# Normalized cross-covariance attention and a multiplicative FFN: the first batch's loads in another order, the last outputs in two PSUM tiles

## The chip, the cores and the metric

The kernel runs on one core of a Trainium2 chip. The metric is the device time of one execution in microseconds (us). Seven executions of the kernel before the change took 575.99 to 577.0 us, median 576.5. All times in the text are in us unless they are marked ns.

The engines are named as in the profile: PE multiplies matrices (PEld is its loading of weights), DVE and ACT do elementwise work, POOL issues the loads that convert float32 to bfloat16, and SP issues the stores and the transposing transfers. A suffix q (SPq, ACTq) marks an engine's queue of transfers.

## The reference

Four batches (B = 4) of q, k and v, each 5824 x 256 in float32. In outline:

```python
qn = q / (norm(q, axis=1) + 1e-6)          # norm of each of the 256 columns, over 5824 rows
kn = k / (norm(k, axis=1) + 1e-6)
s = kn.transpose(0, 2, 1) @ qn / tau       # 256 x 256 per batch, tau = 1
a = softmax(s, -1)
x = (v @ a).reshape(4 * 5824, 256)
h = (x @ w1) * (x @ w2) @ w3               # w1, w2: 256 x 1024; w3: 1024 x 1024
out = h @ w_out                            # w_out: 1024 x 256
```

So the 256 x 256 matrix a of a batch needs every row of its q and k, and only then can the rows of v be worked on.

## The kernel before

**Algebra and tiles.** The rows of a batch lie on 128 partitions, 45 slots to a partition (5760 rows), and 64 rows are left over. A slot is a 128 x 256 tile. Eight slots make a piece: pieces 0 to 4 are full, piece 5 has 5 slots and, for q and k, the 64 left rows in a sixth slot (LAST = 5), padded with zeros. The kernel folds a into the weights: Wf = a @ [w1, w2] per batch, and W_sb = w3 @ w_out once. For each chunk of 512 rows (c = 0 to 10) and each 128 of the 1024 hidden columns (j = 0 to 7), `emit_ab` makes two matmul groups a and b out of the transposed v and Wf (L424), ACT copies a out of PSUM (L430), DVE multiplies it with b (L439). `emit_out` multiplies the product by W_sb[j] and sums over j in PSUM (L463); at j = 7 ACT and DVE copy the sums out (L483, L484) and SP stores them (L485). Chunk 11 of each batch is small: the 45th slot (128 rows) and the 64 left rows. The left rows of two batches are put together as one 128-row tile, so batches 1 and 3 have two output tiles of 128 x 256 in chunk 11, and batches 0 and 2 have one. In the kernel before both lie in one PSUM tile (L459); ACT copies the first half (L473), DVE the second (L476), and the left rows are stored by two transfers of 64 rows each (L479).

**PSUM.** Tag "ab" has four buffers, tag "out" three, "G" one. A chunk takes two "out" tiles in turn, so a chunk's second tile takes the buffer of the first tile of the chunk before.

**The first batch.** Nothing can run beside it, so its order is written out by hand (L496 to L565). POOL loads the pieces of q and k in the order of `load_piece` calls; each transfer also waits until the one eight places ahead of it has landed. PE makes, per slot, the squares of k (`squares`, L221; the diagonal of k^T k gives k's norms), those of q, and the products G = q^T k (`products`, L233). `busy` issues matmuls on a tile of zeros that nothing reads (L209). The softmax is in units, `soft0`:

- `k_first` (L244): DVE takes the diagonal of k's squares into dk.
- `k_row` (L272 to L277): PE spreads the k norms to a row; ACT makes kr, the inverse norm, in four operations.
- `q_first` (L251): DVE takes the q sums into ss.
- `scaled_first`: DVE scales half of G by kr (L302), ACT and DVE make r from ss (L291 to L294), DVE scales the other half, ACT makes e = exp(r * s) in two operations (L307).
- `first_folds`: PE sums e (L323), DVE makes the inverse rs (L329, L330), and PE makes folds 0 to 5 (L344), 128 x 512 each; ACT evicts the even ones (L351) and DVE the odd ones (L353), scaled by rs, into Wf. Folds 0 to 3 are needed by j = 0 to 3, folds 4 to 7 by j = 4 to 7. Folds 6 and 7 come between the first matmuls of the main loop.

The first half of v's piece 0 is transposed by PE (L132), copied out by DVE (L136), and stands ahead of `first_folds`. After the q and k pieces POOL loads the halves of w1 and w2 (L539, L540) between the halves of v_0, then v_1, v_2, w_out (L546) and w3 (L547).

**Later batches.** Loads, squares, products and softmax of batch n + 1 are spread over batch n by an agenda of due times (`make_agenda`); `gate` and `hold` keep POOL from issuing loads too early.

The functions that the change touches, and what calls them:

Of the kernel before, what the change touches and what calls it, by code (L numbers as in the profile page):

```python
# [12 lines left out]
F32 = DT.float32  # L13
BF16 = DT.bfloat16

P = 128
# [8 lines left out]
def kernel(  # L25
# [12 lines left out]
    nc = tc.nc  # L38

    B, N, C = q.shape  # L40
    T, D = out.shape
# [8 lines left out]
    FT = F // P  # L50
    NT = N // P
    LEFT = N - NT * P
    assert LEFT == 64 and NT % 4 == 1
    NP_ = (NT + PIECE - 1) // PIECE
    LAST = NT - (NP_ - 1) * PIECE
# [11 lines left out]
    work = ctx.enter_context(tc.tile_pool(name="work", bufs=2))  # L67
    psum = ctx.enter_context(tc.tile_pool(name="psum", bufs=1, space=bass.MemoryType.PSUM))
# [16 lines left out]
    W_sb = consts.tile([P, FT, D], BF16)  # L85
# [14 lines left out]
    def new_piece(nm, n, pi):  # L100
        t = in_pool.tile([P, PIECE, C], BF16, tag=nm, name=f"{nm}_{n}_{pi}", bufs=IN_BUFS[nm])
        pieces[nm, n, pi] = t
        if pi == NP_ - 1:
            if nm != "v":
                nc.vector.memset(t[LEFT:, LAST, :], 0.0)
            nc.gpsimd.dma_start(out=t[:LEFT, LAST, :], in_=qk_main[nm, n][1])

    def load_part(nm, n, pi, lo, hi):
        nc.gpsimd.dma_start(  # L109
            out=pieces[nm, n, pi][:, lo:hi, :], in_=qk_main[nm, n][0][:, pi * PIECE + lo : pi * PIECE + hi, :]  # L110
        )

    def load_piece(nm, n, pi, cuts=()):

        new_piece(nm, n, pi)
        ends = [0, *cuts, LAST if pi == NP_ - 1 else PIECE]
        for lo, hi in zip(ends, ends[1:]):
            load_part(nm, n, pi, lo, hi)
# [3 lines left out]
    def new_vT(n):  # L122
        vTs[n] = (
            vT_pool.tile([P, NT - 1, CT, P], BF16, tag="vT", name=f"vT_{n}"),
            vT_pool.tile([P, CT, P + LEFT], BF16, tag="vTt", name=f"vTt_{n}"),
        )
# [11 lines left out]
    def transpose_half_on_pe(n, pi, h, on_act):  # L138
        if pi == 0 and h == 0:
            new_vT(n)  # L140
        t = pieces["v", n, pi]
        i0 = 4 * h
        pe_transpose(
            vTs[n][0][:, pi * PIECE + i0 : pi * PIECE + i0 + 4, :, :].rearrange("p i c t -> p (i c) t"),
            [t[:, i0 + i, ct * P : (ct + 1) * P] for i in range(4) for ct in range(CT)],
            "out", on_act,
        )
# [57 lines left out]
    def busy(k):  # L205

        m = psum.tile([P, 512], F32, tag="ab", name=f"warm_{nc.get_next_instruction_name()}", bufs=4)
        for _ in range(k):
            nc.tensor.matmul(m, lhsT=warm[:, :P], rhs=warm, start=True, stop=True, skip_group_check=True)  # L209
# [3 lines left out]
    def squares(nm, pi, slots, end=False):  # L213

        if nm not in S:
            S[nm] = psum.tile([P, CT, P], F32, tag="out", name=f"sq{nm}_0", bufs=3)
        t = pieces[nm, 0, pi]
        for i in slots:
            for ct in range(CT):
                cs = slice(ct * P, (ct + 1) * P)  # L220
                nc.tensor.matmul(  # L221
                    S[nm][:, ct, :], lhsT=t[:, i, cs], rhs=t[:, i, cs],
                    start=(pi == 0 and i == 0 and ct == 0),
                    stop=(end and i == slots[-1] and ct == CT - 1), skip_group_check=True,
                )

    def products(pi, slots, end=False):
        if 0 not in G_tiles:
            G_tiles[0] = psum.tile([P, CT, C], F32, tag="G", name="G_0", bufs=1)
        qt, kt = pieces["q", 0, pi], pieces["k", 0, pi]  # L230
        for i in slots:
            for ct in range(CT):
                nc.tensor.matmul(  # L233
                    G_tiles[0][:, ct, :], lhsT=qt[:, i, ct * P : (ct + 1) * P], rhs=kt[:, i, :],
                    start=(pi == 0 and i == 0 and ct == 0),
                    stop=(end and i == slots[-1] and ct == CT - 1), skip_group_check=True,
                )

    def soft_units(n):
# [94 lines left out]
            sum_mm(0)  # L334
            sum_mm(1)

        def fold_mm(i, c2, tag="ab"):
            h, rest = divmod(i, 4)
            w, c1 = divmod(rest, 2)
            if c2 == 0:  # L340
                st["fold", i] = psum.tile(
                    [P, 512], F32, tag=tag, name=f"fold_{n}_{i}", bufs={"ab": 4, "out": 3}[tag]
                )
            nc.tensor.matmul(  # L344
                st["fold", i], lhsT=st["e"][:, c2, c1 * P : (c1 + 1) * P], rhs=w12[:, c2, w, h * 512 : (h + 1) * 512],
                start=(c2 == 0), stop=(c2 == CT - 1),
            )
            if c2 == CT - 1:
                dst = Wf[n][:, c1, w, h * 512 : (h + 1) * 512]
                if i % 2 == 0:  # L350
                    nc.scalar.activation(out=dst, in_=st["fold", i], func=AF.Copy, scale=st["rs"][:, c1 : c1 + 1])  # L351
                else:
                    nc.vector.tensor_scalar_mul(dst, st["fold", i], st["rs"][:, c1 : c1 + 1])  # L353

        def fold(i, tag="ab"):
            fold_mm(i, 0, tag)
            fold_mm(i, 1, tag)

        def first_folds():
            sum_mm(0)  # L360
            fold_mm(0, 0)
            fold_mm(1, 0)
            sum_mm(1)
            fold_mm(0, 1)
            fold_mm(1, 1)
            fold(2)
            fold(3)
            fold(4, "out")
            fold(5, "out")

        if n == 0:
# [77 lines left out]
    def emit_out(b, c, j, ab):  # L449
        small = c == NCH - 1  # L450
        if small:
            lhs = [ab[:, :P]]
            if b % 2 == 1:
                lhs.append(lefts[b // 2][:, j, :, :].rearrange("p b t -> p (b t)"))
        else:
            lhs = [ab[:, i * P : (i + 1) * P] for i in range(4)]
        if j == 0:
            out_tiles[b, c] = [
                psum.tile([P, 2, D], F32, tag="out", name=f"o_{b}_{c}_{h}", bufs=3) for h in range((len(lhs) + 1) // 2)  # L459
            ]  # L460
        tl = out_tiles[b, c]
        for s, lhsT in enumerate(lhs):
            nc.tensor.matmul(  # L463
                tl[s // 2][:, s % 2, :], lhsT=lhsT, rhs=W_sb[:, j, :],
                start=(j == 0 and s % 2 == 0), stop=(j == FT - 1 and (s % 2 == 1 or s == len(lhs) - 1)),
                skip_group_check=True,
            )
        clock[0] += len(lhs) * (D * MM_COL + MM_FIX)
        if j == FT - 1:
            o = work.tile([P, 4, D], F32, tag="o_sb", name=f"osb_{b}_{c}", bufs=3)  # L470
            rows = out[b * N : b * N + NT * P, :].rearrange("(p i) c -> p i c", i=NT)
            if small:
                nc.scalar.copy(o[:, 0, :], tl[0][:, 0, :])  # L473
                (nc.scalar if b == B - 1 else nc.sync).dma_start(out=rows[:, NT - 1, :], in_=o[:, 0, :])
                if b % 2 == 1:
                    nc.vector.tensor_copy(o[:, 1, :], tl[0][:, 1, :])  # L476
                    for k in range(2):
                        m = b - 1 + k
                        nc.sync.dma_start(  # L479
                            out=out[m * N + NT * P : (m + 1) * N, :], in_=o[k * LEFT : (k + 1) * LEFT, 1, :]  # L480
                        )
            else:
                nc.scalar.copy(o[:, 0:2, :], tl[0])  # L483
                nc.vector.tensor_copy(o[:, 2:4, :], tl[1])  # L484
                nc.sync.dma_start(out=rows[:, 4 * c : 4 * c + 4, :], in_=o)  # L485
            del out_tiles[b, c]
# [8 lines left out]
    half = PIECE // 2  # L495
# [20 lines left out]
    for pi in range(1, 4):  # L516
        load_piece("k", 0, pi)
        load_piece("q", 0, pi)
    load_piece("k", 0, 4)
    load_piece("k", 0, 5)  # L520
    soft0 = soft_units(0)
    whole = range(PIECE)
# [6 lines left out]
        products(0, sl)  # L529
    for pi in range(1, 4):  # L530
        squares("k", pi, whole)
        busy(2)
        squares("q", pi, whole)
        products(pi, whole)
    load_piece("q", 0, 4, (half,))
    load_piece("q", 0, 5, (2, 4))
    for h in range(2):
        hs = slice(h * F // 2, (h + 1) * F // 2)
        nc.gpsimd.dma_start(out=w12[:, :, 0, hs], in_=w1r[:, :, hs])  # L539
# [6 lines left out]
    nc.gpsimd.dma_start(out=wout_sb, in_=moe_w_out.rearrange("(lh ll) c -> ll lh c", ll=P))  # L546
    nc.gpsimd.dma_start(out=w3_bf, in_=w3r)  # L547
    squares("k", 4, whole)
    squares("k", 5, range(LAST + 1), end=True)
    soft0[0]()  # L550
    busy(2)
    soft0[1]()
    for sl in (lo, hi):
        squares("q", 4, sl)
        products(4, sl)
    parts = [[LAST, 0, 1], [2, 3], [4]]
    for sl in parts:
        squares("q", 5, sl, end=sl is parts[-1])
        if sl is parts[-1]:
            soft0[2]()  # L560
        products(5, sl, end=sl is parts[-1])
    soft0[3]()
    busy(4)
    transpose_half_on_pe(0, 0, 0, False)
    soft0[4]()  # L565
    w_ready = [False]

# [114 lines left out]
```

## Time and profile before

| | us |
|---|---|
| median of seven executions | 576.5 |
| the profiled execution, whole time | 577.43 |
| its span, first to last recorded instruction | 575.7 |
| PE busy | 562.2 (98%) |
| DVE, ACT, POOL busy | 374.5, 338.2, 65.1 |
| first matmul of the main loop (L424) | near 40.5 |
| last output matmul ends | 571.16 |
| last store issued | near 572.6 |

How to read the lines: a row in order of time gives start, duration, engine, line of the kernel, operation, output <- input with shapes, the number of instructions merged (x12), and in brackets how long the engine sat idle just before and what ended that. In a list of waits a row gives who waited for whom, the sum in us, how often, and the longest. A row of the chain of waits gives start, duration and the group that set the time. In the DMA view a queue's row gives packets, MB, and the time of its packets as a share of 16 engines over the window; an issue's row gives KB each and the us from issue to landing.

### The profile page before, as it was taken

To read this page: it belongs to the slowest core of one execution; us is meant where nothing else is said; L and a number is where in the kernel's file an instruction comes from. 1 tells how busy PE (TensorE), PEld (TensorE's weight loads), DVE (VectorE), ACT (ScalarE), POOL (GpSimd) and SP (SyncE) were. 2 spreads that over 40 slices of the span, in tenths; PEclk is the share of its full clock that TensorE was granted. 3 is DMA by queue.
4 is the path that set the end of the run, shared out by engine and by line. 5 is a ranking of instruction groups with operands and counts; after the bars stand their busy time and mean duration, and the time that the engine had idled before them with its cause. 6 is when DMAs were issued, how large, how long until landed. Compare 5 with 4: busy or idle time off the path is not lost.

```text
span 575.7 us, 10111 instructions
## 1 busy us (share of the span) xinstructions
PE 562.2 (98%) x3762; PEld 357.3 (62%) x3770; DVE 374.5 (65%) x597; ACT 338.2 (59%) x624; POOL 65.1 (11%) x147
## 2 busy tenths in 40 slices
PE   8799999999999999999999999999999999999996
PEld 4665576776666566666666666666665656566665
DVE  0047744787967567887776567778876656565564
ACT  0046534777766477776765567767765554454453
POOL 5240020202100111011000112001100000000000
PEclk9999999999999999999999999999999999999999
DMA  8999969969571999564642799654563335311011
GB/s 164 211 208 199 185 112 217 186 159 223 129 176 47 139 176 210 113 145 93 144 110 77 149 215 178 147 111 88 147 138 81 84 79 145 84 41 71 38 74 55
DMA packets 74416, 76.93 MB, mean 134 GB/s; under 512 B 54144, under 2 KB 58112, under 8 KB 74368
## 3 DMA queue, kind: packets, MB, share of 16 engines
q0 software_dynamic: 15360, 39.46, 39.9%
q1 hardware_dynamic: 58864, 36.71, 22.6%
q8 instruction: 29, 0.48, 0.4%
q14 instruction: 19, 0.16, 0.1%
q10 hardware_dynamic: 144, 0.13, 0.1%
HBM read 78.91 MB, written 23.86 MB: 179 GB/s over the span
## 4 chain that ended last, share of the span: by engine, by line
PE 88%; DMA 7%; ACT 1%; issue 1%; DVE 1%; POOL 1%; ACTq 0%; POOLq 0%
PE a L424 27%; PE o L463 26%; PE b L424 26%; PE G L188 5%; DMA q<-in_q_dram 4%; DMA k<-in_k_dram 2%; PE fold L344 2%; PE w L571 1%; DMA v<-in_v_dram 1%; ACT as L430 1%; POOL k L109 0%; DVE abs L439 0%; DVE osb L484 0%; PE row L272 0%; POOL q L109 0%
## 5 line engine op out<-in xcount | busy, mean ns | idle before, releaser
L439 DVE TENSOR_TENSOR abs<-as,b 128x512 bf16<-128x512 bf16 x336 | 229.6, 685 | 141.7 <-ACT as L430 130.5
L430 ACT CAST as<-a 128x512 bf16<-128x512 f32 (+1 forms) x384 | 215.4, 562 | 178.1 <-PE a L424 87.7
L424 PEld LDWEIGHTS <-Wf 128*128 128x128 bf16 x1536 | 149.1, 98 | 102.2 <-issue 2.3
L463 PE MATMUL o<-W_sb,abs 128*128 128x256 bf16 x1376 | 209.6, 273 | 0.5 <-ACT osb L483 0.4
L424 PE MATMUL a<-vT,Wf 128*128 128x512 bf16 x704 | 209.3, 379 | 0.4
L424 PE MATMUL b<-vT,Wf 128*128 128x512 bf16 x704 | 209.4, 379 | 0.0
L463 PEld LDWEIGHTS <-abs 128*128 128x128 bf16 x1376 | 134.5, 98 | 82.0 <-issue 0.6
L197 DVE TENSOR_TENSOR acc<-acc,sq 128x1024 f32<-128x1024 f32 x66 | 80.4, 1219 | 0.8 <-ACT sq L185 0.8
L188 PE MATMUL G<-k,q 128*128 128x256 bf16 x276 | 49.6, 273 | 1.1 <-DMA k<-in_k_dram 1.1
L412 POOL COPY gate_t<-abs 1x1 bf16<-1x1 bf16 x39 | 9.7, 248 | 300.7 <-DVE abs L439 292.1
L185 ACT ACTIVATE sq<-q 128x512 f32<-128x512 bf16 x66 | 41.8, 633 | 0.0
L185 ACT ACTIVATE sq<-k 128x512 f32<-128x512 bf16 x66 | 41.6, 630 | 0.0
L484 DVE COPY osb<-o 128x512 f32<-128x512 f32 x44 | 30.1, 684 | 0.0
L188 PEld LDWEIGHTS <-q 128*128 128x128 bf16 x276 | 27.0, 98 | 4.5 <-issue 1.4
L483 ACT COPY osb<-o 128x512 f32<-128x512 f32 x44 | 25.7, 585 | 4.6 <-PE o L463 2.6
L274 ACT ACTIVATE kr<-row 128x256 f32<-128x256 f32 x4 | 1.5, 384 | 31.0 <-PE row L272 31.0
L109 POOL DMA_DIRECT2D q<-in_q_dram x28 | 15.0, 538 | 14.0 <-DMA k<-in_k_dram 5.2
L344 PE MATMUL fold<-w,e 128*128 128x512 bf16 x61 | 16.3, 378 | 0.1
L351 ACT ACTIVATE Wf<-fold,rs 128x512 bf16<-128x512 f32 x16 | 10.9, 687 | 7.2 <-PE fold L344 4.3
L109 POOL DMA_DIRECT2D k<-in_k_dram x25 | 13.8, 551 | 3.4 <-DMA k<-in_k_dram 1.9
L109 POOL DMA_DIRECT2D v<-in_v_dram x25 | 13.4, 540 | 5.7 <-issue 3.9
L439 DVE TENSOR_TENSOR abq<-as,b 128x512 bf16<-128x512 bf16 x16 | 10.9, 686 | 3.9 <-ACT as L430 3.4
(89 smaller groups left out, 209.8 us busy)
## 6 DMA issues: line engine op xcount, KB each, us to landing
out_dram<-osb SPq DMA_DIRECT2D x44, 512.0 KB, 3.1
k<-in_k_dram POOLq DMA_DIRECT2D x19, 512.0 KB, 8.9
v<-in_v_dram POOLq DMA_DIRECT2D x19, 512.0 KB, 5.2
q<-in_q_dram POOLq DMA_DIRECT2D x18, 512.0 KB, 6.8
w_wout<-in_moe_w_dram POOLq DMA_DIRECT2D x1, 2048.0 KB, 22.3
k<-in_k_dram POOLq DMA_DIRECT2D x4, 320.0 KB, 9.0
v<-in_v_dram POOLq DMA_DIRECT2D x4, 320.0 KB, 6.0
q<-in_q_dram POOLq DMA_DIRECT2D x4, 256.0 KB, 10.4
```

What stands on the lines that cost most here:

```text
L109: nc.gpsimd.dma_start(out=pieces[nm, n, pi][:, lo:hi, :], in_=qk_main[nm, n][0][:, pi * PIECE + lo : pi * PIECE + hi, :])
L185: nc.scalar.activation(out=dst[:, :, part, :], in_=src[:, o : o + 2, :], func=AF.Square)
L188: nc.tensor.matmul(G[:, ct, :], lhsT=qt[:, i, ct * P : (ct + 1) * P], rhs=kt[:, i, :], start=(pr == 0 and part == 0 and ct == 0), stop=(pr ...
L197: nc.vector.tensor_add(accs[n], accs[n], sqs[0])
L344: nc.tensor.matmul(st["fold", i], lhsT=st["e"][:, c2, c1 * P : (c1 + 1) * P], rhs=w12[:, c2, w, h * 512 : (h + 1) * 512], start=(c2 == 0), ...
L351: nc.scalar.activation(out=dst, in_=st["fold", i], func=AF.Copy, scale=st["rs"][:, c1 : c1 + 1])
L424: nc.tensor.matmul(t[:, :n], lhsT=Wf[b][:, ct, w, j * P : (j + 1) * P], rhs=rhs_of(b, c, ct), start=(ct == 0), stop=(ct == CT - 1),)
L430: nc.scalar.copy(a_sb[:, :n], tiles[0][:, :n])
L439: nc.vector.tensor_mul(ab, a_sb, tiles[1])
L463: nc.tensor.matmul(tl[s // 2][:, s % 2, :], lhsT=lhsT, rhs=W_sb[:, j, :], start=(j == 0 and s % 2 == 0), stop=(j == FT - 1 and (s % 2 == 1 ...
L483: nc.scalar.copy(o[:, 0:2, :], tl[0])
L484: nc.vector.tensor_copy(o[:, 2:4, :], tl[1])
```

## The change

Five edits in the first batch, and two at the outputs of the small chunk:

1. q_4 is loaded and used ahead of k_5 (before: k_4, k_5, q_4, q_5). The pieces alternate to the end.
2. q_5 comes in four parts and not three (slots 0; 1 and 2; 3; 4; the left rows ahead of them), and its squares and products are made in the parts [LAST, 0], [1, 2], [3], [4].
3. `k_row` stands behind the first of these parts; before it stood ahead of q_4.
4. Two pairs of `busy` matmuls go: after the squares of k_3, and between `k_first` and `k_row`.
5. The PE transposes of v's first half move from ahead of `first_folds` to between folds 2 and 3. Fold 3 is evicted by ACT and fold 4 by DVE (before the other way round).
6. In chunk 11 of batches 1 and 3 the two output tiles take a PSUM tile each.
7. The left rows are copied into an SBUF tile of their own and stored by one transfer on SP, 128 rows, whose destination is two groups of 64 rows; before there were two transfers. The 45th slot's store of the last batch is on ACT's queue as before.

```diff
@@ first_folds
             fold_mm(0, 1)
             fold_mm(1, 1)
             fold(2)
-            fold(3)
-            fold(4, "out")
+            transpose_half_on_pe(0, 0, 0, False)
+            fold(3, on_act=True)
+            fold(4, "out", on_act=False)
             fold(5, "out")
@@ emit_out
-                psum.tile([P, 2, D], F32, tag="out", name=f"o_{b}_{c}_{h}", bufs=3) for h in range((len(lhs) + 1) // 2)
+                psum.tile([P, 2, D], F32, tag="out", name=f"o_{b}_{c}_{h}", bufs=3)
+                for h in range(len(lhs) if small else 2)
             ]
         tl = out_tiles[b, c]
         for s, lhsT in enumerate(lhs):
+            h, o = (s, 0) if small else divmod(s, 2)
             nc.tensor.matmul(
-                tl[s // 2][:, s % 2, :], lhsT=lhsT, rhs=W_sb[:, j, :],
...
+                tl[h][:, o, :], lhsT=lhsT, rhs=W_sb[:, j, :],
...
                 if b % 2 == 1:
-                    nc.vector.tensor_copy(o[:, 1, :], tl[0][:, 1, :])
-                    for k in range(2):
-                        m = b - 1 + k
-                        nc.sync.dma_start(
-                            out=out[m * N + NT * P : (m + 1) * N, :], in_=o[k * LEFT : (k + 1) * LEFT, 1, :]
-                        )
+                    o2 = work.tile([P, D], F32, tag="kr", name=f"oleft_{b}", bufs=1)
+                    nc.vector.tensor_copy(o2, tl[1][:, 0, :])
+                    pair = out.rearrange("(b n) c -> b n c", n=N)[b - 1 : b + 1, NT * P :, :]
+                    nc.sync.dma_start(out=pair, in_=o2)
@@ the first batch
     load_piece("k", 0, 4)
+    load_piece("q", 0, 4, (half,))
     load_piece("k", 0, 5)
...
         squares("k", pi, whole)
-        busy(2)
+        if pi < 3:
+            busy(2)
         squares("q", pi, whole)
         products(pi, whole)
-    load_piece("q", 0, 4, (half,))
-    load_piece("q", 0, 5, (2, 4))
+    load_piece("q", 0, 5, (1, 3, 4))
...
     squares("k", 4, whole)
-    squares("k", 5, range(LAST + 1), end=True)
-    soft0[0]()
-    busy(2)
-    soft0[1]()
     for sl in (lo, hi):
         squares("q", 4, sl)
         products(4, sl)
-    parts = [[LAST, 0, 1], [2, 3], [4]]
-    for sl in parts:
-        squares("q", 5, sl, end=sl is parts[-1])
-        if sl is parts[-1]:
+    squares("k", 5, range(LAST + 1), end=True)
+    soft0[0]()
+    parts = [[LAST, 0], [1, 2], [3], [4]]
+    for i, sl in enumerate(parts):
+        end = i == len(parts) - 1
+        squares("q", 5, sl, end=end)
+        if end:
             soft0[2]()
-        products(5, sl, end=sl is parts[-1])
+        products(5, sl, end=end)
+        if i == 0:
+            soft0[1]()
     soft0[3]()
     busy(4)
-    transpose_half_on_pe(0, 0, 0, False)
     soft0[4]()
```

`soft0[0]` to `soft0[4]` are the units `k_first`, `k_row`, `q_first`, `scaled_first` and `first_folds`. `fold` and `fold_mm` get an argument `on_act` that says which engine evicts.

## The prediction

> **What bounds the kernel now.** I read the page first (busy shares, then the chain that ended last), then TensorE's waits after its main loop starts, then the order of time in the two places that the change touches, and last the DMA view of the end.
>
> ```profile
> PE 562.2 (98%) x3762; PEld 357.3 (62%) x3770; DVE 374.5 (65%) x597; ACT 338.2 (59%) x624; POOL 65.1 (11%) x147
> PE 88%; DMA 7%; ACT 1%; issue 1%; DVE 1%; POOL 1%; ACTq 0%; POOLq 0%
> ...
> PE G L188 <- DMA k<-in_k_dram: 1.1, 1, 1.1
> PE o L463 <- ACT osb L483: 0.4, 1, 0.4
> ```
>
> PE is 98% busy and is 88% of the chain. From 40 us on it waits 1.7 us in all, so whatever start and end give or take goes straight into the time. The start, in order of time:
>
> ```profile
> 28.81 0.84 PE L221 MATMUL sqk<-k 128*128 128x128 bf16 x12 [0.49 <-DMA k<-in_k_dram]
> ...
> 29.69 0.42 DVE L244 TENSOR_TENSOR dk<-sqk,ident 128x256 f32<-128x256 f32 x1 [18.00 <-PE sqk L221]
> ...
> 30.91 0.38 ACT L274 ACTIVATE kr<-row 128x256 f32<-128x256 f32 x1 [28.89 <-PE row L272]
> ...
> 31.71 0.70 POOL L539 DMA_DIRECT2D w<-in_moe_w_dram  x1 [0.86 <-DMA q<-in_q_dram]
> ...
> 35.00 0.28 PE L221 MATMUL sqq<-q 128*128 128x128 bf16 x2
> ...
> 36.33 0.56 DVE L293 TENSOR_SCALAR r<-r 128x2 f32<-128x2 f32 x1 [0.17 <-ACT r L292]
> ...
> 37.12 0.91 ACT L307 ACTIVATE e<-s,r 128x256 bf16<-128x256 f32 x2 [0.83 <-DVE r L294]
> 37.68 0.11 PEld L323 LDWEIGHTS <-e 128*128 128x128 bf16 x2 [0.18 <-ACT e L307]
> ...
> 37.06 0.63 PE tr_I-494_495 L132 x8
> ...
> 38.37 2.18 PE fold L344 x10
> ```
>
> After k_5 lands (28.8), PE works without a gap until 35.2, so the last q norms come from PE's backlog and not from a transfer. The first sums at 37.68 wait for ACT's e; the v transposes of 37.06 lie in front of that wait and cost nothing. And the end:
>
> ```profile
> 571.19 0.37 ACT L473 COPY osb<-o 128x256 f32<-128x256 f32 x1 [0.83 <-PE o L463]
> 571.59 0.37 ACTq L474 DMA_DIRECT2D out_dram<-osb  x1
> 571.59 0.42 DVE L476 COPY osb<-o 128x256 f32<-128x256 f32 x1 [0.78 <-ACT osb L473]
> 572.04 1.12 SPq L479 DMA_DIRECT2D out_dram<-osb  x2
> ...
> q10 hardware_dynamic: 144, 0.13, 3.5%
> ...
> out_dram<-osb ACTq DMA_DIRECT2D x1, 128.0 KB, 1.7
> out_dram<-osb SPq DMA_DIRECT2D x2, 64.0 KB, 2.0
> ```
>
> DVE's copy waits for ACT's copy of the same PSUM tile, then SP issues two stores one after the other. The last three lines are the DMA view of 565 to 576 us.
>
> **Start, q_4 before k_5.** The bytes up to k_5's landing in the new order are those up to q_4's second half in the old. The queue's issue at 31.71 waited for that landing; on k_5's landing the same kind of issue came at 29.05 and PE at 28.81, so PE starts 0.24 before it: k_5's squares now start at 31.47. From there, with old distances: squares of k_5 0.63 (28.81 to the next load at 29.44), slots LAST and 0 of q_5 0.66: 32.76. dk ends at 31.47+0.84+0.04+0.42 = 32.77; the row starts 0.06 later, 32.83. The next squares start 0.54 after a row (30.17 to 30.71): 33.37; slots 1, 2 and 3 take 0.99, and slot 4's squares run 34.36 to 34.64. dq starts at 34.67, against 35.31: 0.64 earlier.
>
> **The row among the q pieces.** From the row's start (30.17) to the end of ACT's four kr operations (32.73) it is 2.56 us: 35.39. Before, that was 3 us ahead of its reader; now kr is later than the q sums (34.67+0.43 = 35.10), and ACT runs r's Ln behind kr. So r starts at 35.39 and not 35.85, and the whole 0.64 does not come through: e is 0.46 earlier, 36.66.
>
> **The transposes behind fold 2.** They leave the place that e covered and enter PE's chain: 8 take 0.45 (the second group stands in the chain of waits with 0.45). 0.46 - 0.45: the first main-loop matmul stays at 40.5. Their copy on DVE (0.69) ends near 40.0. Fold 3 goes to ACT, ending at 40.46, before its reader at 41.1; folds 4 and 5 on DVE end at 41.6, where the first product waits for ACT anyway (41.64). No gain, no loss there; if a copy came late, PE would stand still for what is missing.
>
> I bound the start by one row. r's TENSOR_SCALAR took 562 ns, the other three of its kind 169 or 170; it ran 36.33 to 36.89, and POOL's DMA issue of L547 ran 36.04 to 36.92. The change moves it to 35.85, into or between POOL's issues of 0.90 and 0.88. Unhindered the start gains 0.4; held until a second issue ends near 37.1 it loses 0.7. I take 0, the case of one such hold as now. The Trainium skill (SBUF — State Buffer, Who interferes with whom) says that VectorE's two-port operations, tensor_scalar among them, and GpSimd shut each other out for whole instructions; taken as certain to hit the second issue, that rule would make the start 0.7 slower, while by three rows of four it gains.
>
> **q_5 in four parts.** One more POOL issue (0.53). POOL sat idle 0.5 to 3.3 before most of the issues in question, and each waits for the transfer eight places ahead of it, so the queue stays full and landings follow the bytes. v_0's first half is issued up to 1.4 later (30.31 waited for q_4, now for k_5), still ahead of some 3 us of queued bytes, and is now read 2 us after its old landing (37.01). The second w1 part, 256 KB at 212 GB/s after that, lands near 38.2; fold 4 reads it at 39.6. Last on this queue, w3 slips by up to 0.5; its readers start at 66.90, after transposes issued from 58.45 on. If these covers went, PE would wait up to 0.5.
>
> **The two pairs of warm matmuls** left out lay in PE's waits for q_3 (23.6 to 24.6) and for dk: nothing. PE idles there for 1 us; it idled 2.1 us before q_2 and the granted clock stayed at 1.00 in that window.
>
> **Two PSUM tiles for the small chunk** (batches 1 and 3). The second tile takes the buffer of the chunk before, so its first matmul waits for ACT's copy. At the end that copy runs 566.81 to 567.39 and the matmul stands at 567.43: between 0 and 0.1, twice; I take 0.05 in all.
>
> **The end.** DVE no longer waits for ACT: 571.19 to 571.61, SP issues at 571.64. Before, the second issue started near 572.58 and landed 2.0 later, 574.58; the span ends 1.1 after that. So the new store breaks even if it lands within 2.94 us of its issue. How long does it take? Its destination is walked as 2 x 64 rows of 1 KB. No row shows a store with so small a leading count, so I bound it. Queue q10 holds ACT's store: 3.5% of 16 engines over 11 us is 6.2 us for 128 packets, 48 ns each. Eight per engine are 0.4 us of its 1.7, so 1.3 is fixed. Spread over all 16 engines the new store lands in 1.7 to 2.3 (2.3 is the slowest 128 KB store in the run): end faster by 0.6 to 1.2. On one engine: 1.3 + 128 x 0.048 = 7.4, slower by 4.5. I assume that it is dealt out by its leading count, two ways, because both kinds of store in the trace have leading counts (64, 128) that 16 divides and so say nothing for this one: 1.3 + 64 x 0.048 = 4.4, 0.1 more for L479's slower issue (0.56 against 0.33), 4.5. The end moves by 4.5 - 2.94: 1.56 slower. In batch 1 the same store ends near 326; SP's next transfer there is issued at 327.35, so nothing waits.
>
> The Trainium skill speaks for both sides here. DMA: Bandwidth & Descriptors (Rules for kernel authors) advises one 128-partition transfer in place of two halves, which is this edit. The same page (Why a DMA increments its semaphore by 16 and not by 1) says that the engines used are the largest number up to 16 that divides the slowest dimension of both sides, here 2 and 128, so two. By its 27 GiB/s per engine 64 KB take an estimated 2.3 us, the store 3.6 us, and the end would be 0.7 slower.
>
> **Sum.** Start 0, middle +0.05, end +1.56: 1.6. The profiled execution took 577.43 (span 575.7): 579.0 after. It stands 0.9 above the median of 576.5, so the median goes to 578.1.
>
> **Rivals.** (1) The other side: the store uses all engines. The end gains 0.9 (a landing in 2.0), the total is 576.5 - 0.85 = 575.65. For it: every 128 KB store so far landed in 2.3 or less. Against: none has this shape. It decides at a landing under 2.94. (2) r is held by POOL's second issue: +0.7 on top, 578.8. For it: the 562 ns; against: three of four are not held. (3) One engine: 576.5 + 4.55 = 581.05. For it: only that no row excludes it. (4) The start gains 0.4 because r is not held, with two engines: 577.7; for it the three rows at 170 ns.
>
> **Numbers.** Forecast with (4): 0.60. (1): 0.25. (2): 0.12. (3): 0.03. Within 0.2% (1.15 us) is about what a measurement can't tell from no change. Slower by more: (2), (3) and 0.52 of the forecast, 0.67; the forecast's other 0.08 is a landing under 4.1 and lies within. Of (1) 0.17 lies within; 0.08 is faster, where the start gains too (under 575.35). So faster 0.08, within 0.25, slower 0.67. The range 575.6 to 579.2 leaves out half of (1) below and (3) above; the forecast's own is 577.3 to 579.0.
>
> **What would show it.** Row, kr and e: dq near 34.7, r behind kr at 35.4, e near 36.7, first main-loop matmul still near 40.5. DVE's last copy level with ACT's at 571.2 or the same shift, one SP issue, and its landing: 4.5 us is right, 2 us is rival 1. Wrong would be k_5 landing later than 31.5, or a store whose engines take 1 KB packets faster than 48 ns.

## The result and the profile after

The changed kernel took 581.84 us (median of 12 executions, 579.34 to 588.18), the kernel before 576.45 beside it (median of 30). The ratio of the means, without the execution of 588.18, is 1.0111, 95% interval 1.0086 to 1.0136: slower, as forecast, but by 5.4 us at the median and not by 1.6, and above the forecast range. The executions fall into two groups: seven from 579.3 to 582.7, five from 587.0 to 588.2. The kernel before has no such second group (575.99 to 577.42).

The profiled execution took 579.62, with a span of 577.8. It belongs to the faster group, so its profile can't show everything. Its page, first the busy times and then the shares of the chain that ended last:

```profile
PE 561.5 (97%) x3760; PEld 356.7 (62%) x3766; DVE 374.4 (65%) x597; ACT 338.0 (58%) x624; POOL 65.0 (11%) x148
PE 88%; DMA 8%; ACT 1%; issue 1%; POOL 1%; DVE 1%; ACTq 0%; POOLq 0%
```

PE's work is the same (561.5 against 562.2): nothing was added to it. What grew stands around it. TensorE's waits in the changed kernel, from 40 us on, with the sum, the count and the longest:

```profile
PE G L188 <- DMA k<-in_k_dram: 1.2, 1, 1.2
PE o L466 <- ACT osb L484: 0.4, 1, 0.4
```

The list has almost the same numbers as before, and that is a trap. Before, the wait for k was at 200.7 us; it is gone, or at most 0.3, in the profiles of the change and of its variants. Now it is at 334 us, in front of batch 3's first products, a place where the kernel before had no wait for k in its profile. The start of the changed kernel, in order of time:

```profile
31.37 0.84 PE L221 MATMUL sqk<-k 128*128 128x128 bf16 x12 [0.20 <-DMA k<-in_k_dram]
...
32.25 0.42 DVE L244 TENSOR_TENSOR dk<-sqk,ident 128x256 f32<-128x256 f32 x1 [21.05 <-PE sqk L221]
...
34.57 0.29 DVE L251 CUSTOM_DVE_ANT_0 dq<-sqq,ident 128x128 f32<-128x128 f32 x1 [1.89 <-PE sqq L221]
...
34.87 0.42 ACT L277 ACTIVATE kr<-kr 128x256 f32<-128x256 f32 x1
35.12 0.95 POOL L548 DMA_DIRECT2D w_wout<-in_moe_w_out_dram  x1
...
35.66 0.40 DVE L293 TENSOR_SCALAR r<-r 128x2 f32<-128x2 f32 x1
...
36.30 0.91 ACT L307 ACTIVATE e<-s,r 128x256 bf16<-128x256 f32 x2 [0.68 <-DVE r L294]
...
39.39 0.55 PEld L344 LDWEIGHTS <-e 128*128 128x128 bf16 x4 [0.58 <-DMA w<-in_moe_w_dram]
```

e starts at 36.30, 0.82 earlier than before. Most of it is given back behind e, and the last line shows one cause: the second half of w1 lands at 39.35, and the weight load of the next fold waits for it. The chain of waits of this stretch ends in the first main-loop matmul (L425):

```profile
32.15 7.21 DMA w<-in_moe_w_dram
39.35 0.05 issue
39.40 1.04 PE fold L344 x4
40.44 0.43 PE a L425 x2
```

40.44 against 40.55 before: the start is worth 0.1 in this profile. From the first sums, 36.86 now and 37.69 before, to this matmul it takes 3.58, and it took 2.86. Of the 0.72 more, 0.45 are the transposes and 0.27 the wait for w1: the 0.58 in the last row is idle time of PEld, which loads weights ahead, while PE was still busy with earlier folds. The end, in order of time, and below it what SP waits for after its last issue:

```profile
571.03 0.28 PE L466 MATMUL o<-W_sb,left 128*128 128x256 bf16 x1
571.22 0.37 ACT L476 COPY osb<-o 128x256 f32<-128x256 f32 x1 [0.70 <-PE o L466]
571.35 0.42 DVE L480 COPY oleft<-o 128x256 f32<-128x256 f32 x1 [0.38 <-PE o L466]
571.62 0.37 ACTq L477 DMA_DIRECT2D out_dram<-osb  x1
571.80 0.57 SPq L482 DMA_DIRECT2D out_dram<-oleft  x1
```

```profile
SPq L679 <- DMA out_dram<-oleft: 3.3, 1, 3.3
SPq L679 <- DMA out_dram<-osb: 0.8, 1, 0.8
```

The two copies now run side by side and the stores are issued within 0.2 us of each other. But SP waits 0.8 for ACT's store and then 3.3 more for its own: 571.80 + 0.57 + 0.8 + 3.3 is a landing at about 576.5, 4.7 after the issue. From the end of PE's last matmul to the end of the span it is now 6.49, and it was 4.55: the end costs 1.94. The DMA view of 571 to 578 us says why (40 slices of 0.175 us, the digit is the busy share of 16 engines in tenths, then the queues with packets, MB and share):

```profile
DMA  0000000029811011111101011111110000000000
...
q1 hardware_dynamic: 130, 0.13, 6.2%
q10 hardware_dynamic: 144, 0.13, 5.7%
```

After ACT's store has landed (the 2, 9, 8) one tenth of the engines works for 3.5 us. Both queues moved 128 packets of 1 KB. ACT's has 16 more, SP's 2 more; if each engine that takes part closes its share with one packet, ACT's store ran on 16 engines and SP's on 2. SP's packets took 6.2% of 16 engines for 7 us, 6.9 us: 54 ns each, and 64 of them on each of two engines are 3.5 us.

That is 1.94 at the end and 1.2 in front of batch 3, 3.1 together, and 579.62 is 3.2 above the median of before. (The profiled execution of before, 577.43, had the 1.1 at 200.7 us in it.) What lifts five of twelve executions to 587 is not in this profile.

### The profile page after: what moved, and what is told of

Read it like the earlier page. It is cut to its first block, busy times and chain, and to the rows that moved or that the text cites. A ratio compares the mean times of both kernels' runs of the same rounds, so it can differ in the third digit from the quotient of the medians.

```text
span 577.8 us, 10103 instructions
## 1 busy us (share of the span) xinstructions
PE 561.5 (97%) x3760; PEld 356.7 (62%) x3766; DVE 374.4 (65%) x597; ACT 338.0 (58%) x624; POOL 65.0 (11%) x148
## 4 chain that ended last, share of the span: by engine, by line
PE 88%; DMA 8%; ACT 1%; issue 1%; POOL 1%; DVE 1%; ACTq 0%; POOLq 0%
PE a L425 26%; PE o L466 26%; PE b L425 26%; DMA k<-in_k_dram 6%; PE G L188 5%; PE fold L344 2%; DMA w<-in_moe_w_dram 1%; PE w L573 1%; ACT as L431 1%; POOL q L109 0%; POOL k L109 0%; DVE abs L440 0%; DVE osb L485 0%; PE row L272 0%; PE ss L283 0%
## 5 line engine op out<-in xcount | busy, mean ns | idle before, releaser
L425 PEld LDWEIGHTS <-Wf 128*128 128x128 bf16 x1536 | 149.1, 98 | 102.5 <-issue 2.6
L425 PE MATMUL a<-vT,Wf 128*128 128x512 bf16 x704 | 209.4, 379 | 0.4
L425 PE MATMUL b<-vT,Wf 128*128 128x512 bf16 x704 | 209.4, 379 | 0.0
L109 POOL DMA_DIRECT2D k<-in_k_dram x25 | 13.8, 551 | 3.7 <-DMA k<-in_k_dram 1.9
```

What stands on the lines that cost most here:

```text
L109: nc.gpsimd.dma_start(out=pieces[nm, n, pi][:, lo:hi, :], in_=qk_main[nm, n][0][:, pi * PIECE + lo : pi * PIECE + hi, :])
L425: nc.tensor.matmul(t[:, :n], lhsT=Wf[b][:, ct, w, j * P : (j + 1) * P], rhs=rhs_of(b, c, ct), start=(ct == 0), stop=(ct == CT - 1),)
```

## The experiments

Theory A: the leading count of the new store's destination, two, puts it on two engines; it costs time at the end and, in batch 1, by holding back loads that use the same engines. Theory B: the edits of the start cause the slow group, by gaps that let PE's clock fall. Theory C: the second PSUM tile makes a wait in batches 1 and 3. The first four runs take the change apart. Their kernel before took 576.33 (27 executions).

**All of the change but the store's form.** The left rows go out by two transfers of 64 rows from the new tile, in both batches:

```diff
-                    pair = out.rearrange("(b n) c -> b n c", n=N)[b - 1 : b + 1, NT * P :, :]
-                    nc.sync.dma_start(out=pair, in_=o2)
+                    for k in range(2):
+                        m = b - 1 + k
+                        nc.sync.dma_start(
+                            out=out[m * N + NT * P : (m + 1) * N, :], in_=o2[k * LEFT : (k + 1) * LEFT, :]
+                        )
```

> The changed kernel, with the left rows of batches 1 and 3 stored as before by two transfers of 64 rows (out of the new SBUF tile). Theory A, the paired store of 2 x 64 rows is slow because of its leading count of 2, and hurts twice: at the end, and after batch 1, where it is still under way when k_0 of batch 3 is loaded and PE waits for that (1.2 us in the profiled run of the change, more in the executions of 586 to 588 us). Then both go: 575.3 to 576.3 us, executions within 1.5 us of each other, no wait of PE for k near 334 us, the end 0.4 shorter than before the change (DVE copies beside ACT). Theory B, the edits of the start make the scatter (PE idles longer there, the mean granted clock of the slow executions was 0.992 against 0.998): executions still scatter over 8 us, only some 2 us lower, 577 to 586. Theory C, the second PSUM tile is what hurts: unchanged, 579 to 588.

Measured: 576.14 (575.83 to 577.01), ratio 0.9996, 0.9987 to 1.0005. The whole loss is gone and so is the slow group, with the start edits and the two PSUM tiles still in. B and C fall; what is left is the form of one store in two places. From the end of PE's last matmul to the end of the span it is 4.10 here, 0.45 less than before the change, as expected.

**The new store in batch 3 alone.**

```diff
+                    if b == B - 1:
                         pair = out.rearrange("(b n) c -> b n c", n=N)[b - 1 : b + 1, NT * P :, :]
                         nc.sync.dma_start(out=pair, in_=o2)
+                    else:
+                        for k in range(2):
...
```

> The changed kernel, with the paired store only in batch 3 (at the end) and two transfers of 64 rows in batch 1. Theory A: the end stays 1.9 longer than before the change, the wait of PE for k after batch 1 goes and the scatter with it: 577.5 to 578.5 us, executions within 1.5 us. Theory B or C: 579 to 588 as in the change.

Measured: 578.61 (578.18 to 578.89), ratio 1.0034, 1.0021 to 1.0046. The end alone costs 2.3 us by the medians and 2.0 by the ratio, with a close spread in five executions; the median is 0.1 above the expected range. SP's wait at the end of this kernel is the same as in the change:

```profile
SPq L686 <- DMA out_dram<-oleft: 3.3, 1, 3.3
```

**The new store in batch 1 alone.** The same edit with `if b < B - 1`.

> The changed kernel, with the paired store only in batch 1 and two transfers of 64 rows in batch 3. Theory A: the end is 0.4 shorter than before the change, and PE waits for k after batch 1 as in the change, 1.2 us in some executions and 8 or so in others: 576.5 to 586 us, scattered. Theory B: the same scatter. So this one and the one with the pair in batch 3 alone tell A from B together: under A they differ in scatter, under B they don't.

Measured: 577.55 (577.0 to 580.4), ratio 1.0022, 1.0011 to 1.0033: 1.2 us. TensorE's waits from 300 to 345 us show the load that pays:

```profile
PE G L188 <- DMA k<-in_k_dram: 0.9, 1, 0.9
```

Batch 1's store, issued at 321.1, costs time 13 us later, through another queue. None of these 11 executions is near 587: the scatter up to 586 that was expected did not come. So 2.3 and 1.2 make 3.5, which is the faster group of the change (median 580.06, 3.6 above the kernel before), and not its median.

**The first batch's edits alone**, with the old outputs:

```diff
-                tl[h][:, o, :], lhsT=lhsT, rhs=W_sb[:, j, :],
-                start=(j == 0 and o == 0), stop=(j == FT - 1 and (small or o == 1)),
+                tl[s // 2][:, s % 2, :], lhsT=lhsT, rhs=W_sb[:, j, :],
+                start=(j == 0 and s % 2 == 0), stop=(j == FT - 1 and (s % 2 == 1 or s == len(lhs) - 1)),
...
-                    nc.sync.dma_start(out=pair, in_=o2)
+                    for k in range(2):
...
```

> The kernel before, with the edits of the first batch alone (order of q_4 and k_5, four parts of q_5, the row, warm matmuls, transposes behind fold 2); the outputs are those of the kernel before. Theory A: no scatter, the first main-loop matmul 0.1 earlier as in the change's profile, 575.9 to 576.5 us. Theory B: executions scatter over 8 us at a granted clock under 0.996.

Measured: 576.21 (575.65 to 576.88), ratio 0.9994, 0.9985 to 1.0002. The new order of the first batch is worth nothing that can be measured.

**The changed kernel again**, unaltered, to see whether the slow group is the program's or belonged to one chip. Beside it the kernel before took 576.13 (23 executions), which is also the measure of the two runs after it.

> The changed kernel once more, unaltered, beside kernels that differ in one edit, on their chip. The pair in batch 1 alone cost 1.2 us (ratio 1.0022) and ranged to 580.4; the pair in batch 3 alone cost 2.3. If the two costs only add, 579.3 to 580.5 us with single executions to 583, and no cluster near 587. If the cluster near 587 belongs to the program, it is seen here again, and the profile may show where its 8 us lie.

Measured: 580.95 (579.08 to 586.7), ratio 1.0102, 1.0061 to 1.0142; of six executions two are near 586. The slow group is the program's, and the sum of the parts does not hold on every execution. The profiled one, 581.78, shows the first step beyond the faster group. PE in order of time:

```profile
335.19 0.38 PE L188 MATMUL G<-k,q 128*128 128x256 bf16 x2 [2.07 <-DMA k<-in_k_dram]
...
335.97 1.06 PE L425 MATMUL b<-vT,Wf 128*128 128x512 bf16 x2
...
339.46 0.60 PE L466 MATMUL o<-W_sb,abs 128*128 128x256 bf16 x4
```

The wait for k is 2.07 now, and after it the same matmul pairs that otherwise take 0.59 take 1.06, for some 3.5 us. The granted clock of 336 to 340 us was 0.61 of full speed.

**One transfer with a leading count of 64.** If it is the count and not "one transfer instead of two", then a single 128-row store whose destination is walked as 64 x 2 rows should lose nothing. The left rows are interleaved in the tile, row first and batch second:

```diff
-                lefts[b // 2] = work.tile([P, FT, 2, LEFT], BF16, tag="left", name=f"left_{b}", bufs=1)
-            nc.vector.tensor_mul(lefts[b // 2][:, j, b % 2, :], a_sb[:, P:n], tiles[1][:, P:n])
+                lefts[b // 2] = work.tile([P, FT, LEFT, 2], BF16, tag="left", name=f"left_{b}", bufs=1)
+            nc.vector.tensor_mul(lefts[b // 2][:, j, :, b % 2], a_sb[:, P:n], tiles[1][:, P:n])
...
-                    pair = out.rearrange("(b n) c -> b n c", n=N)[b - 1 : b + 1, NT * P :, :]
+                    pair = out.rearrange("(b n) c -> n b c", n=N)[NT * P :, b - 1 : b + 1, :]
```

> The changed kernel, with the left rows of the two batches interleaved on the partitions (row, then batch), so that the same single transfer of 128 rows has a destination of 64 x 2 rows and not of 2 x 64. Same bytes, same packets of 1 KB, same queue, one issue. Theory A (the leading count 2 decides): it lands about 2.0 us after its issue and not 4.7, the end is 0.9 shorter than before the change, and PE doesn't wait for k after batch 1: 575.2 to 575.9 us. Rival (one transfer of 128 rows to two places is slow in itself): it lands after 4 us or more, and the time stays near 579 to 580.

Measured: 575.68 (575.36 to 577.37), ratio 0.9995, 0.9987 to 1.0004. The DMA view of the end, 570 to 576 us, in this kernel:

```profile
q1 hardware_dynamic: 144, 0.13, 6.2%
...
out_dram<-oleft SPq DMA_DIRECT2D x1, 128.0 KB, 2.1
```

The same bytes are now 144 packets and land 2.1 after the issue. From the end of PE's last matmul to the end of the span it is 3.78 here, 4.55 before, and 6.43 to 6.55 in all profiles with the 2 x 64 store at the end. The expected landing and time came; PE's wait for k after batch 1 is not quite gone, it is 0.2. The two DMA views of 315 to 335 us (slices of 0.5 us) compare batch 1, first the change, then this kernel:

```profile
DMA  6980100000399499999389999999999922122699
```

```profile
DMA  9951000000697389989999999999999900079999
```

In the second line the engines finish together, at 331, and go idle until the next loads. In the first they go down to one or two tenths and stay there for 2.5 us: most engines have finished their share of the loads, and a few have not. k_0, 512 KB, is complete only with the last of them. That the store is still among them is seen by its packets. They have 1 KB, the packets of the loads 4 KB and those of SP's transposing transfer under 512 B, so they are the difference between two counts in the DMA view of 328 to 333 us, again first the change, then this kernel:

```profile
DMA packets 594, 0.61 MB, mean 122 GB/s; under 512 B 458, under 2 KB 478, under 8 KB 594
```

```profile
DMA packets 622, 0.50 MB, mean 99 GB/s; under 512 B 533, under 2 KB 533, under 8 KB 622
```

20 packets of the store pass in these 5 us in the change, the last three between 332 and 333, though it was issued at 320.32. In this kernel, as in the kernel before (470 and 470), none does. The chain of waits gives k_0's time from issue to landing, in this kernel, and in the change:

```profile
323.30 10.20 DMA k<-in_k_dram
```

```profile
323.47 11.13 DMA k<-in_k_dram
```

**The same with folds 4 and 5 later**, to try for a version that beats both: the wait for w1 stood in front of fold 4, which only j = 4 needs, so folds 4 and 5 go between the first main-loop matmuls like 6 and 7.

```diff
-            fold(4, "out", on_act=False)
-            fold(5, "out")
...
-            return [k_first, k_row, q_first, scaled_first, first_folds] + [lambda i=i: fold(i) for i in range(6, 8)]
+            return [k_first, k_row, q_first, scaled_first, first_folds] + [lambda i=i: fold(i, "out") for i in range(4, 8)]
...
-            for i in range(2):
-                at(1.5 + 0.6 * i, 0.43, soft0[5 + i])
+            for i in range(4):
+                at(0.3 + 0.9 * i, 0.43, soft0[5 + i])
```

> The one with the 64 x 2 store, and folds 4 and 5 of the first batch moved out of the burst to between the first main-loop matmuls, as folds 6 and 7 are. In the change's profile PE waited 0.6 us for the second part of w1 ahead of fold 4. Theory: this wait ends last at the start; without it the first main-loop matmul starts near 39.6 and not near 40.5, the two folds cost their 0.87 of PE later, and the whole is 0.4 to 0.6 under the 64 x 2 store alone: 574.7 to 575.4 us. Rival (ACT or DVE is too busy with the evictions in the first chunk): no gain over the 64 x 2 store, or a loss of up to 0.5.

Measured: 576.0 (575.54 to 576.68), ratio 0.9996, 0.9988 to 1.0005. PE in order of time (its L423 is the change's L425):

```profile
39.61 0.59 PE L423 MATMUL a<-vT,Wf 128*128 128x512 bf16 x2 [0.35 <-DVE vT L136]
```

The first matmul comes at 39.61, but it waits 0.35 for DVE's copy of the transposed v, and the two folds cost their 0.87 later: 40.48 in all, against 40.08 in the same row of the kernel with the folds in front. The gain expected was not there to be had: the 0.6 was PEld's idle time, and PE lost 0.27 by that wait in the change and, by the same sum, 0.18 in the kernel with the 64 x 2 store. The rival's "no gain" is what came.

**The changed kernel three times more**, unaltered, one execution each, to catch the slow group under the profiler.

> The changed kernel once more, for its trace. In the profile of 581.8 us PE waited 2.1 us for k_0 of batch 3 and then ran at half clock from 335.4 to 339. What makes the executions of 586 to 588? If it is the same mechanism, a trace of that kind shows a longer wait or a second wait for loads after batch 1's paired store, each of more than 2 us followed by some 3.5 us at half clock, and the rest of the trace as in the executions of 579. If it is another one, the lost time lies elsewhere.

> The changed kernel once more, for its trace, with the same question: a longer wait or a second wait near 335 us, or time lost elsewhere.

> The changed kernel once more, for its trace, with the same question: a longer wait or a second wait near 335 us, or time lost elsewhere.

Measured: 587.3, 579.65 and 579.83. k_0 lands 11.13 and 11.44 us after its issue in the last two. In the first, by the chain of waits:

```profile
323.23 16.10 DMA k<-in_k_dram
```

The first is of the slow group. PE in order of time, and under it the stretch from 340 to 344 us (busy time of PE, PEld, DVE, ACT and POOL, the granted clock, the DMA share, GB/s):

```profile
339.37 0.59 PE L188 MATMUL G<-k,q 128*128 128x256 bf16 x2 [6.15 <-DMA k<-in_k_dram]
339.75 1.06 PE L425 MATMUL a<-vT,Wf 128*128 128x512 bf16 x2
...
344.44 1.06 PE L466 MATMUL o<-W_sb,abs 128*128 128x256 bf16 x4
...
345.77 0.59 PE L425 MATMUL b<-vT,Wf 128*128 128x512 bf16 x2
```

```profile
340.00:344.00 4.00, 4.00 (x13) 1.82 (x12) 0.69 (x1) 1.29 (x3) 0.00 (x0) 0.50 1.36 78
```

PE stands still for 6.15 us and then works at half clock from 339.75 to 345.8. The matmuls of that stretch, at the 0.43 to 0.44 that each such group takes elsewhere and 0.22 for G, are 3.25 us and took 6.0, so 2.8 is lost. With the wait's 4.9 beyond the usual 1.2 that makes 7.7, and 587.3 - 579.6 is 7.7. The execution of 587.3 has the same wait as batch 1's 1.2 us, with a later landing and half clock after it. In the five profiled executions of the change the wait is 1.2, 1.2, 1.5, 2.07 and 6.15, and the times are 579.62, 579.65, 579.83, 581.78 and 587.3. The other seven executions near 586 to 588 have no trace; that they are of this kind is inferred from their times.

## Why the prediction was right and wrong

**What bounds it: right.** PE's work stayed the same, and the two waits that the change added, 1.94 at the end and 1.2 in front of batch 3, went into the time undiminished (2.3 and 1.2 in the runs with one of them).

**The start, q_4 before k_5 and the row among the q pieces: right, to 0.1.** Squares of k_5 at 31.37 (31.47 predicted), dq at 34.57 (34.67), kr ending at 35.29 (35.39).

**r: the hold was seen again, at a smaller size.** r's TENSOR_SCALAR took 0.40 and ended at 36.06, as POOL's issue of L548 ended (36.07); before, it took 0.56 and ended with POOL's L547, too. The hold was the first issue's and not the second's, so rival 2 did not come about, and r came 0.36 earlier than I took. Ten of the twelve profiles show such an end. In the run with two stores it took 0.16 at 35.41, inside POOL's issue of 35.22 to 36.12, so a hold for a whole instruction, as I cited it, does not fit that row.

**The transposes, and w1 behind q_5's four parts: zero was right, by terms that cancel, which is luck.** e gained 0.82 and not 0.46. The transposes took their 0.45. Against the rest stands a step that failed: "The second w1 part, 256 KB at 212 GB/s after that, lands near 38.2; fold 4 reads it at 39.6." It landed at 39.35, and with e earlier fold 4 came to it sooner: 0.27 lost, which I had costed as covered. The 0.4 of rival 4 was there, on e; this cover took most of it. The 0.1 that is left can't be told from nothing: in the profiles with these edits the first main-loop matmul's row lies between 39.91 and 40.60, and before at 40.39.

**The warm matmuls and the two PSUM tiles: right as far as shown**, nothing and at most 0.1; no run has either alone, but with both in place and the store in its old form the kernel stands at 0.9996.

**The end: right in mechanism, a little small in size.** Two engines, a landing 4.7 after the issue (4.5 predicted), 54 ns a packet (48), 1.94 in the profile and 2.0 to 2.3 in the run with that edit alone, against 1.56. Rival 1 (all 16 engines) and rival 3 (one) both fall, by 130 packets and 4.7 us. The Trainium skill's rule (DMA: Bandwidth & Descriptors, Why a DMA increments its semaphore by 16 and not by 1), that the number of engines is the largest up to 16 that divides the slowest dimension of both sides, agrees with 130 packets for a count of 2 and with 144 for 64. The end that I worked out from its rate per engine, 0.7 slower, is less than half of what was measured.

**Batch 1: wrong, and this is the step that failed:** "In batch 1 the same store ends near 326; SP's next transfer there is issued at 327.35, so nothing waits." Neither half held. I took the landing from the end of the run, where only ACT's store moves beside it: 4.5 after the issue. But the profile before shows the two halves of the same store landing 5.8 after their issue there, and not 2.0 as at the end. Its DMA view of 315 to 330 us:

```profile
k<-in_k_dram POOLq DMA_DIRECT2D x1, 512.0 KB, 10.0
...
out_dram<-osb SPq DMA_DIRECT2D x2, 64.0 KB, 5.8
```

The new store's packets pass until 333, 12 us after the issue. And I looked only at the queue behind the store. POOL's loads of v_0, q_0 and k_0 for batch 3, issued 1 us before to 3 us after it, share the engines. With the store's share beside it on two engines k_0 lands 10.8 to 16.1 us after its issue, where it took 9.8 to 10.2 in the six kernels without the 2 x 64 store in batch 1, and PE reads it 10 us after its issue: there was no slack. That alone is 1.2 us. In part of the executions k_0 comes 2 to 6 us late and half clock follows. This makes the scatter of the profiled executions and, if the rest of the slow group is like its one trace, the 2.2 us by which the median lies above the 579.62 of the first profile. My prediction had no term and no rival for it, which is why the range was too low, and none of its signs of being wrong points there.

**What stays open.** Why k_0's landing varies between 11 and 16 us from one execution to the next. The store's own share is 3.5 us on each of two engines, and 16.1 us is 6 more than undisturbed, so the store's bytes alone do not account for it. A rival that no run tests is the transposing transfer of v_0, which SP issues near 327, behind the store. It landed 23.7 us after its issue in the execution of 587.3, 17.4 in the one of 581.78, 13.2 to 13.8 in the three others, and 10.1 to 13.0 in the kernels without the 2 x 64 store in batch 1. In the execution of 587.3 the store's packets are all through before 335, but from 336 to 341 POOL's loads get only 16 packets through (161 in the change's first profile), beside 1101 of SP's queue. On the other side, the store in batch 1 alone had 17.3 at a wait of 0.9, so the two do not go in step, and which of the transfers holds up the other is not shown. The store in batch 1 alone showed no execution near 587 in 11, while the whole change showed 8 in 21: whether that is chance, needs the other edits or hangs on the chip (13 there, 11 and 4 in the repeats) was not settled. None of the versions beats the kernel before: the best median, 575.68 against 576.13, has 1 within its interval.

## What to carry to other kernels

Before two stores are made one, look at the outermost count that the merged access has on both sides: 2 x 64 rows ran on two engines and took 4.7 us, 64 x 2 rows on all and took 2.1. A transfer on few engines is not paid for in its own queue alone; go through every load of every queue that is in flight beside it, and look at how much time lies between that load's landing and its reader. Take the store's own landing from the place where it stands, not from a quiet one. For PE, 98% busy here, a late load can cost more than its lateness: behind the two longest waits the clock was at half.

## What the runs showed of the hardware

**Half clock came after waits of 2.07 and 6.15 us, but not after every wait of 2 us.** Waits for k of 0.9, 1.2 and 1.5 us were followed by matmuls at full clock. After 2.07 us the granted clock was 0.92, 0.50 and 0.72 in the three stretches of 2 us from 334, which is half clock for 3.4 us; after 6.15 us it was 0.64, 0.50, 0.50 and 0.65 in the four from 338, half clock for 6.8 us. In the kernel before, PE stood idle for 2.12 us until 20.05, and the granted clock stayed at 1.00, so the length of the wait alone does not decide. The Trainium skill (TensorE: Matmul & The Clock Gate, Part 1: The HAM clock gate) has half clock come after an idle window of about 3.4 us that runs freely, and full clock after a window as long. The 3.4 and 6.8 us at half clock agree; that 2.07 us of standing still was enough is less than the page's figure.

**One short store moved a load on another queue by 1 to 6 us**, although the store carries 128 KB and the load 512, and it did so unevenly: the same program on the same chip gave 11.1, 11.4 and 16.1 us for the same load.
